# Hash bits for attention masked on TensorE: four 32-column products instead of two full ones, 32-row mask products, and the first weights fetched by SP

## The chip, the cores and the metric

The kernel runs on one core of one Trainium2 chip (trn2). A core has a matrix engine (TensorE, PE in the profile; PEld are its weight loads), a vector engine (VectorE, DVE), an activation engine (ScalarE, ACT), a general engine (GpSimd, POOL) and an engine that mostly issues DMAs (SyncE, SP). Each works through its own queue in order and waits on semaphores for the others. On-chip memory is SBUF (128 partitions); products land in PSUM (128 partitions, in banks).

The metric is device time in microseconds, the median of several runs. The time before the change is 1106.46 us (9 runs, 1104.96 to 1110.92).

## The reference, cut to what matters

Attention with a hash mask, followed by a Fourier mixing block and a two-layer network. Shapes: q, k, v are 4 x 8 x 768 x 64 in float32, `proj` is 64 x 6, the two weights are 512 x 2048 and 2048 x 512 in float64.

```python
q_bits = (np.einsum('bhsd,dk->bhsk', q, proj) > 0)      # 6 bits per query
k_bits = (np.einsum('bhsd,dk->bhsk', k, proj) > 0)      # 6 bits per key
mask = q_bucket[:, :, :, None] == k_bucket[:, :, None, :]  # all six bits equal
scores = np.where(mask, scale * q @ k.T, -1e9)
attn = softmax(scores); x = attn @ v                       # then heads side by side
mixed = np.real(fft(fft(x, axis=1), axis=2))
u = x + mixed
out = u + np.maximum(layernorm(u) @ w_ch1, 0.0) @ w_ch2
```

## The kernel before

**Tiling.** Two heads make a pair, one on partitions 0 to 63 and one on 64 to 127 (a head has 64 dimensions). There are 4 batches of 4 pairs, numbered n = 0 to 15. Queries and keys are 768 long: six tiles of 128 keys (`c`, 0 to 5), and two halves of 384 queries (`g`, `HALF` = 384).

**One key tile.** `weigh(n, c)` makes, for each half g, the scores of both heads in one PSUM tile of two banks (`sc`): products of `kt` and `qt` over 64 partitions for each head (line 869). ACT then takes the exponential into `pk` (line 873). `values` multiplies `pk` of the tile before with v (line 890), and DVE adds up `pk` for the row sums (line 964). At the end of a pair `scale` forms the sums by 32-column products (`sum`, line 908) and divides.

**The mask, in two ways.** Pairs in `LITE` (n = 0 to 4) are masked on TensorE: for each half and head a bf16 product over the hash bits (line 862) is put into the same PSUM tile first, and the scores are added to it. The bits of q are +-0.5 with one more row of -1.5, those of k are +-0.5 with a row of 1, and q's are multiplied by 2^34, so that the sum is 0 where all six bits agree and hugely negative otherwise. Later pairs (n from 5) turn the bits into a bucket number by small products (lines 804, 818, 828), and DVE compares the numbers after the exponential (line 879).

**Bits of a lite pair.** `prepare(n)` runs one pair ahead, a step per key tile. For q and for k, and for each half of the sequence, it multiplies `pjw` (128 x 128, the projection of head h in rows and columns from 64 h) with the transposed input (line 789), and DVE turns the result into bits of both heads, on partitions 0.. and 64.. (line 791; for q also line 796). The tile `qk` holds q's 768 columns and k's 768 columns.

**PSUM buffers.** Products outside the scores and values take a buffer by `pt`. In the first prologue it goes through several pools; afterwards only `ps_1`, with two buffers, serves (line 521). The bits (line 789), the column sums of weights (`ws`, line 656, and `wm`, line 664) and the row sums (line 908) all take turns in these two.

**Weights.** The first weight arrives in float64, as 16 slices of 512 KB. `weights1` converts one slice per key tile in four of five steps: DVE lines 631, 635 and 641, ACT lines 639, 646 and 647. Seven slices are fetched ahead by SP; each further one is fetched into the slot just converted, by POOL (line 701, `Arrival.convert`). Some converted columns are averaged on PE (`ws`, ACT's copy `part` of line 661, `wm`) and centred on DVE (line 670).

**Order of the work.** In batch 0 the order of PE, DVE, ACT and POOL is the order of the program (`manual_schedule`, line 1457). SP's order, and everything later, is set by a scheduler. From batch 1 on, mixing and the network of the batch before (`cs`, `A`, `B`, `un`, `h_p`, `o`) are put between the key tiles. SP also loads q, k and v of the next pair (lines 556, 562, 570), q in eight and k in four transfers of 128-byte pieces.

Of the kernel before, what the change touches and what calls it, by code (L numbers as in the profile page):

```python
# [14 lines left out]
I64 = mybir.dt.int64  # L15
U32 = mybir.dt.uint32
AF = mybir.ActivationFunctionType
ALU = mybir.AluOpType
AX = mybir.AxisListType

P = 128
# [3 lines left out]
DFF = 4 * DM  # L25
# [24 lines left out]
def _consts():  # L50


    s = np.arange(HALF)
    freq = np.concatenate([2 * np.arange(NK), 2 * np.arange(NK) + 1])
    ang = 2.0 * np.pi * (np.outer(s, freq) % S) / S
    seq = np.stack([np.cos(ang), np.sin(ang)])
    seq = seq.reshape(2, NT // 2, P, 2 * NK).transpose(2, 0, 1, 3)


    d = np.arange(DM // 2)  # L60
    ang = 2.0 * np.pi * (np.outer(d, np.arange(DM)) % DM) / DM
    sin = -np.sin(ang)
    sin[0] = 1.0 - 2.0 * (np.arange(DM) % 2)
    chan = np.concatenate([np.cos(ang), sin]).reshape(NDC, P, DM).transpose(1, 0, 2)

    off = np.zeros((P, 2))
    for h in range(2):
        off[h * D : h * D + NBITS] = 0.5  # L70
        off[h * D + NBITS] = (NBITS / 4.0, -1.0)


    pw = np.zeros((P, 2, P))
    for r in range(P):
        h, bit = divmod(r % 32, NBITS)
        if h < 2:
            pw[r, h] = 2.0**bit


    d = np.arange(DM // 2)
    fr = np.concatenate([np.arange(DM // 2 + 1), np.arange(1, DM // 2)])
    ang = 2.0 * np.pi * (np.outer(d, fr) % DM) / DM
    ch = np.where(np.arange(DM) <= DM // 2, np.cos(ang), np.sin(ang))
    ch = ch.reshape(2, P, DM // 2, 2).transpose(1, 0, 3, 2)

    s = np.concatenate([np.arange(2, HALF // 2, 2), np.arange(1, HALF // 2, 2)])  # L90
    rows = np.concatenate([s, [0, HALF // 2], s])
    kind = np.repeat([0, 1, 2, 3], [len(s), 1, 1, len(s)])
    sq = np.zeros((2, 2, P, HALF + 1))
    for par in range(2):
        cols = slice(par * NK, HALF + 1 if par else NK)
        ang = 2.0 * np.pi * (np.outer(rows, freq[: HALF + 1][cols]) % S) / S
        for k in range(2):
            own = kind == (0 if par == k else 3)
            own |= (kind == 1) & (k == 0) | (kind == 2) & (k == par)
            w = np.where(own[:, None], np.sin(ang) if k else np.cos(ang), 0.0)  # L100
            w = w.reshape(NT // 2, P, -1)
            sq[0, k, :, cols] = w[0 if par == k else 2]
            sq[1, k, :, cols] = w[1]
    sq = sq.transpose(2, 0, 1, 3)
    return {
        "pw": np.ascontiguousarray(pw, dtype=np.float32),
        "ch": np.ascontiguousarray(ch, dtype=np.float32),
        "sq": np.ascontiguousarray(sq, dtype=np.float32),
        "seq": np.ascontiguousarray(seq, dtype=np.float32),
        "chan": np.ascontiguousarray(chan, dtype=np.float32),  # L110
        "off": np.ascontiguousarray(off, dtype=np.float32),
    }

# [366 lines left out]
def _main(  # L480
# [27 lines left out]
    def wt(shape, dtype, tag, name, bufs=2):  # L508
        return work.tile(shape, dtype, tag=tag, name=name, bufs=bufs)
# [4 lines left out]
    def pt(shape, name):  # L514

        turn[0] += 1
        if roomy[0] and turn[0] % 2:
            if turn[0] % 4 == 1:
                return ps_o.tile(shape, F32, tag="o", name=name)
            return ps_sc.tile(shape, F32, tag="sc", name=name)  # L520
        return ps_1.tile(shape, F32, tag="ps", name=name)
# [62 lines left out]
    for h in range(2):  # L584
        nc.sync.dma_start(pjw[h * D : (h + 1) * D, h * D : h * D + NBITS], proj)
    off = const.tile([P, 2], F32, tag="off", name="off")
    nc.sync.dma_start(off, cn["off"].ap())
    load(0, "v")
    pj = const.tile([P, 32], F32, tag="pj", name="pj")
    nc.gpsimd.memset(pj, 0.0)  # L590
# [81 lines left out]
    class Arrival:  # L672


        def __init__(self, slices, raws, col):
            self.slices, self.raws, self.col = slices, raws, col
            self.wide = slices[0][1].dtype == I64
            self.depth = len(raws) if self.wide else 4

        def fetch(self, i, queue):  # L680
            if i < len(self.slices):
                dst, src = self.slices[i]
                if self.wide:
                    raw = self.raws[i % self.depth].bitcast(I32)
                    queue.dma_start(raw.bitcast(I64), src)
                else:
                    n = dst.shape[-1]
                    queue.dma_start(
                        dst, src if len(dst.shape) == 2 else src.rearrange("p (s n) -> p s n", n=n)
                    )  # L690

        def convert(self, i, low=None):
            if self.wide:
                dst = self.slices[i][0]
                raw = self.raws[i % self.depth].bitcast(I32)
                if len(dst.shape) == 2:
                    raw = raw.rearrange("p (n w) -> p n w", w=2)
                else:
                    raw = raw.rearrange("p (s n w) -> p s n w", w=2, n=dst.shape[-1])
                narrow(dst, raw, self.col + i, low)  # L700
            self.fetch(i + self.depth, nc.gpsimd)

    def weights1():
        slices = [
            (w1[:, c, f : f + WC], moe_w_ch1[c * P : (c + 1) * P, f : f + WC])
            for f in range(0, DFF, WC)
            for c in range(NDC)
        ]
        zt = wt([P, 3, 2 * WC], F32, "z", "zraw1", 1)
        ft = wt([P, 12, WC], F32, "F", "fraw", 1)  # L710
        raws = [zt[:, i] for i in range(3)] + [
            ft[:, i : i + 2].rearrange("p i w -> p (i w)") for i in range(0, 8, 2)
        ]
        arrival = Arrival(slices, raws, 0)
        for i in range(arrival.depth):
            arrival.fetch(i, nc.sync)
            if i == 1:
                load(1)
        yield
        half = None  # L720
        for i in range(len(slices)):
            arrival.convert(i, ft[:, 8 + i % 4].bitcast(I32))
            yield
            if half:
                centre(half[0], next(half[1]))
                half = None
            if i % NDC == NDC - 1:


                f = i // NDC * WC  # L730
                if f < DFF // 2:
                    half = f, average(f)
                    next(half[1])
# [13 lines left out]
    def prepare(n):  # L747
# [33 lines left out]
        if lite:  # L781


            qk = wt([P, 2, S], BF16, "qb", f"qkb{n}")
            for io, nm in enumerate("qk"):
                for g in range(2):
                    cols = slice(g * HALF, (g + 1) * HALF)
                    ps = pt([P, HALF], f"bits{nm}{n}_{g}")
                    nc.tensor.matmul(ps, pjw, ts[nm][:, cols], start=True, stop=True)
                    bits = qk[:, io, cols]  # L790
                    nc.vector.tensor_scalar(
                        bits, ps, 0.0, off[:, io : io + 1],
                        op0=ALU.is_gt, op1=ALU.subtract,
                    )
                    if io == 0:
                        nc.vector.tensor_scalar(bits, bits, BIG, None, op0=ALU.mult)
                yield
            preps[n] = ts["q"], ts["k"], qk, None
            return
# [50 lines left out]
    def weigh(n, c):  # L850
# [6 lines left out]
        for g in range(2):  # L857
            qs = slice(g * HALF, (g + 1) * HALF)
            ps = ps_sc.tile([P, 2, 512], F32, tag="sc", name=f"sc{n}_{g}_{c}")
            if kb is None:  # L860
                for h, rows in enumerate(heads):
                    nc.tensor.matmul(
                        ps[:, h, 0:HALF], qb[rows, 1, ks], qb[rows, 0, qs],
                        start=True, stop=False,
                    )

            for h, rows in enumerate(heads):
                with behind() if g + h and n >= NPAIR else nullcontext():
                    last[0] = nc.tensor.matmul(  # L869
                        ps[:, h, 0:HALF], kt[rows, ks], qt[rows, qs],  # L870
                        start=kb is not None, stop=True,
                    )
            nc.scalar.activation(  # L873
                pk[:, g, :, 0:HALF], ps[:, :, 0:HALF], AF.Exp, scale=SCALE
            )
# [313 lines left out]
    def weights2():  # L1189

        slices = []
        for half in range(2):
            for r in range(HF // 2):
                for hi, first in ((0, B11), (1, B21)):
# [5 lines left out]
                        (dst[:, first : first + step + 1 : step, r],  # L1200
                         moe_w_ch2[c * P : (c + 1) * P, :])
                    )
        arrival = Arrival(slices, [zt2[:, i] for i in range(2)], NDC * DFF // WC)
        for half in range(2):
            for i in range(arrival.depth) if half == 0 else ():
                arrival.fetch(i, nc.gpsimd)
            for i in range(HF):
                arrival.convert(half * HF + i)
                yield
# [360 lines left out]
```

## Time and profile before

| | |
|---|---|
| median of 9 runs | 1106.46 us |
| the profiled execution | 1105.14 us |
| its span on the core | 1103.4 us |
| mean granted TensorE clock | 0.994 |
| mask products (line 862) | 120, median 323 ns, 11.9 to 155.6 us |
| bits of lite pairs on PE (line 789) | 40 records (two passes a product), median 486 ns |
| evictions of bits on DVE (line 791) | 20, some 0.61 us each |
| scaling of q's bits (line 796) | 10, 0.26 us each |
| weight fetches by POOL (line 685), up to 67.5 us | 9, 0.53 to 0.77 us of POOL each |

A profile is one execution. Its page gives busy time by engine, groups of equal instructions by source line, and the chain of waits that ended last. A timeline row gives the start, the length, the engine, the line, the operation, output and inputs, the shape and the number of merged instructions; brackets give the idle time ahead of the first of them and what ended it. A float32 product appears as two passes. On PE a pass is pipelined: its length includes a tail during which the next one already streams, so what it occupies is read from start to start. "128*32" is the part of the array in use, rows by columns.

### The profile page before, as it was taken

The page shows a single profiled execution, that of the slowest core. Times are in us where ns is not written, and L with a number is a line of the kernel's source. Part 1 is how long each engine was busy: PE and PEld are TensorE (multiplying, and loading weights), DVE is VectorE, ACT ScalarE, POOL GpSimd, SP SyncE. Part 2 cuts the span into 40 slices and gives each one's busy share as a digit, 9 for nine tenths or more (in the row PEclk, how much of TensorE's full clock was granted, in tenths as well). Part 3 has the DMA queues.
Part 4 walks back from the last instruction along what each step waited for, and adds up shares of the span by engine and source line. Part 5 has one row for each costly group of instructions (what it writes and reads, how often), then busy time and mean ns, then how long its engine had stood idle before and what let it go on. Part 6 is the DMA issues. An engine that isn't in the chain of part 4 may idle for free.

```text
span 1103.4 us, 14065 instructions
## 1 busy us (share of the span) xinstructions
PE 1048.8 (95%) x4893; PEld 636.5 (58%) x4893; DVE 790.3 (72%) x1326; ACT 499.6 (45%) x1055; POOL 63.1 (6%) x141
## 2 busy tenths in 40 slices
PE   6989898999989999999999999999999999999996
PEld 3334354445744675545664576645674569768675
DVE  5889968868598977786768785975856785644353
ACT  6978566554267324354426424354315532340420
POOL 1000000002000020010000011001000002100000
PEclk9999999999999999999999999999999999999999
DMA  9845434351055161313144134213032205122401
GB/s 225 210 91 121 81 106 105 119 176 26 20 134 187 66 190 53 63 59 75 26 153 109 49 67 167 44 38 91 20 113 80 66 29 172 53 82 83 127 20 42
DMA packets 175567, 103.13 MB, mean 93 GB/s; under 512 B 129408, under 2 KB 162816, under 8 KB 175488
## 3 DMA queue, kind: packets, MB, share of 16 engines
q1 hardware_dynamic: 168400, 83.93, 28.9%
q0 software_dynamic: 5520, 17.83, 5.3%
q8 instruction: 41, 0.67, 0.3%
q10 hardware_dynamic: 1568, 0.39, 0.2%
q14 instruction: 38, 0.31, 0.1%
HBM read 81.14 MB, written 20.97 MB: 93 GB/s over the span
## 4 chain that ended last, share of the span: by engine, by line
PE 57%; DVE 8%; ACT 3%; issue 1%; DMA 1%; DVEq 0%; ACTq 0%
PE o L1246 20%; PE h_p L1366 19%; PE oo L890 6%; PE sc L869 5%; PE cs L1062 2%; DVE pk L879 2%; PE A L1091 2%; PE B L1091 1%; DVE acc L964 1%; ACT rr L924 1%; DMA zraw<-in_moe_w_ch_dram 1%; PE un L1117 1%; DVE w L1258 1%; PE bits L804 1%; DVE h L1232 1%
## 5 line engine op out<-in xcount | busy, mean ns | idle before, releaser
L1246 PE MATMUL o<-w,h 128*128 128x256 f32 x1152 | 259.4, 382 | 1.1 <-ACT tq L1265 0.7
L1246 PEld LDWEIGHTS o<-w,h 128*128 128x128 f32 x1152 | 216.3, 190 | 43.5 <-issue 4.6
L873 ACT ACTIVATE pk<-sc 128x768 f32<-128x768 f32 x192 | 147.9, 808 | 80.5 <-PE sc L869 62.0
L1366 PE MATMUL h_p<-x,w 128*128 128x384 f32 x448 | 163.5, 495 | 3.9 <-ACT h L1388 2.3
L890 PE MATMUL oo<-pk,vn 128*64 128x385 f32 (+1 forms) x768 | 156.0, 501 | 3.8 <-DVE pk L879 3.3
L869 PE MATMUL sc<-qt,kt 64*128 64x384 f32 x768 | 153.5, 502 | 3.3 <-ACT pk L873 3.0
L879 DVE SCALAR_TENSOR_TENSOR pk<-qb,kb,pk 128x768 f32<-128x768 bf16 x132 | 129.1, 1014 | 29.1 <-ACT pk L873 29.0
L1366 PEld LDWEIGHTS h_p<-x,w 128*128 128x128 f32 x448 | 82.4, 190 | 71.8 <-ACT pk L873 5.4
L964 DVE TENSOR_TENSOR acc<-acc,pk 128x1536 f32<-128x1536 f32 (+1 forms) x72 | 105.9, 1484 | 6.6 <-ACT pk L873 6.1
L1366 PE MATMUL h_p<-w 128*128 128x384 f32 x288 | 105.5, 489 | 2.3 <-ACT w L1403 2.3
L890 PEld LDWEIGHTS oo<-pk,vn 128*64 128x64 f32 x768 | 49.5, 136 | 97.6 <-issue 70.6
L869 PEld LDWEIGHTS sc<-qt,kt 64*128 64x128 f32 x768 | 66.4, 186 | 48.3 <-issue 24.3
L1366 PEld LDWEIGHTS h_p<-w 128*128 128x128 f32 x288 | 53.7, 190 | 41.7 <-ACT w L1403 3.5
L1258 DVE SCALAR_TENSOR_TENSOR w<-o,rs,w 128x256 f32<-128x256 f32 x56 | 26.8, 481 | 41.6 <-PE o L1246 41.6
L1276 ACT COPY tq<-o 128x256 f32<-128x256 f32 x24 | 8.9, 372 | 105.3 <-PE o L1246 105.3
L1246 PE MATMUL o<-w 128*128 128x256 f32 x176 | 42.3, 383 | 1.3 <-DVE w L1258 1.3
L1392 DVE TENSOR_TENSOR h<-h 128x384 f32<-128x384 f32 x32 | 17.8, 556 | 32.7 <-ACT h L1391 32.7
L1265 ACT COPY tq<-o 128x256 f32<-128x256 f32 x24 | 8.9, 371 | 69.3 <-PE o L1246 69.3
L1000 POOL DMA_DIRECT2D out_dram<-w x30 | 16.3, 546 | 388.5 <-issue 293.2
L1246 PEld LDWEIGHTS o<-w 128*128 128x128 f32 x176 | 32.8, 190 | 8.8 <-DVE w L1258 2.9
L1399 DVE TENSOR_TENSOR h<-h 128x384 f32<-128x384 f32 x32 | 17.7, 554 | 26.8 <-ACT h L1398 26.8
L1292 DVE TENSOR_TENSOR tq<-tq,o 128x256 f32<-128x256 f32 x24 | 10.0, 419 | 34.7 <-PE o L1246 34.7
(170 smaller groups left out, 1352.2 us busy)
## 6 DMA issues: line engine op xcount, KB each, us to landing
w<-ad SPq DMA_DIRECT2D x168, 128.0 KB, 2.0
w<-bd SPq DMA_DIRECT2D x42, 512.0 KB, 4.5
zraw<-in_moe_w_ch_dram POOLq DMA_DIRECT2D x21, 512.0 KB, 4.2
bd<-w SPq DMA_DIRECT2D x14, 512.0 KB, 4.0
vn<-in_v_dram SPq DMA_DIRECT2D x32, 192.0 KB, 3.6
qn<-in_q_dram SPq DMA_DIRECT2D x120, 48.0 KB, 2.4
kn<-in_k_dram SPq DMA_DIRECT2D x60, 96.0 KB, 3.5
ad<-tq SPq DMA_DIRECT2D x8, 512.0 KB, 3.0
```

What stands on the lines that cost most here:

```text
L869: last[0] = nc.tensor.matmul(ps[:, h, 0:HALF], kt[rows, ks], qt[rows, qs], start=kb is not None, stop=True,)
L873: nc.scalar.activation(pk[:, g, :, 0:HALF], ps[:, :, 0:HALF], AF.Exp, scale=SCALE)
L879: nc.vector.scalar_tensor_tensor(w, qb[:, h].rearrange("p (g s) -> p g s", g=2), kb[:, h, c : c + 1], w, op0=ALU.is_equal, op1=ALU.mult,)
L890: nc.tensor.matmul(oos[g][h * D : (h + 1) * D, 0:w], nat["v", n][:, (2 * c + h) * D : (2 * c + h + 1) * D], pk[:, g, h, 0:w], start=(c == ...
L964: nc.vector.tensor_tensor(acc[:, g], (first if c == 1 else acc)[:, g], new[:, g], op=ALU.add,)
L1062: nc.tensor.matmul(ps[:, pc + 2 * lo : pc + 2 * hi - 1 : 2], z[:, cp, pc, par, t * P : (t + 1) * P], ch[:, cp, pc, lo:hi], start=(cp == 0) ...
L1091: nc.tensor.matmul(ps[:, cols], F[:, par, k, t, j * P : (j + 1) * P], sq[:, t, k, cols], start=(t == 0), stop=(t == 1),)
L1246: nc.tensor.matmul(ps, a[:, r], right7[i][:, r], start=start and r == 0, stop=r == HF // 2 - 1, skip_group_check=not start,)
L1258: nc.vector.scalar_tensor_tensor(t[:, cols], src, r, t[:, cols], op0=ALU.mult, op1=ALU.add)
L1366: nc.tensor.matmul(ps, left[:, k], right[i][:, k], start=start and k == 0, stop=k == 1, skip_group_check=not start,)
L1392: nc.vector.tensor_tensor(c21, c12, c21, op=ALU.add)
L1399: nc.vector.tensor_tensor(c22, c21, c22, op=ALU.add)
```

## The change

Three things change, for the pairs that are masked on TensorE (n = 0 to 4) and for the first weights:

- The bits of q (and in the same way of k) come from four products of 32 columns, one for each half of the sequence and head, into the four quarters of one PSUM tile of 384 columns, instead of from two products of 128 columns in two PSUM tiles. One eviction on DVE serves all four; the table `off` is laid out for this (`off4`).
- The tile `qk` thus has the first half of the sequence on partitions 0 to 63 and the second on 64 to 127, each head on 32. A query half is multiplied on its own 64 partitions, so the keys' bits are needed on both: two copies on DVE bring each half's key bits to the other half's partitions, in columns 384 to 767. A mask product then runs over 32 rows (before: 64), and for g = 1 the key tiles are found at columns turned by three tiles.
- The fetches of the first weights after the first seven are issued by SP instead of POOL. Those of the second weights stay with POOL.

```diff
@@ _consts
+        "off4": np.ascontiguousarray(np.tile(off[:32], (4, 1)), dtype=np.float32),
@@ _main
-    nc.sync.dma_start(off, cn["off"].ap())
+    nc.sync.dma_start(off, cn["off4"].ap())
@@ class Arrival
-        def __init__(self, slices, raws, col):
-            self.slices, self.raws, self.col = slices, raws, col
+        def __init__(self, slices, raws, col, queue):
+            self.slices, self.raws, self.col, self.queue = slices, raws, col, queue
...
-                    queue.dma_start(raw.bitcast(I64), src)
+                    self.queue.dma_start(raw.bitcast(I64), src)
...
-            self.fetch(i + self.depth, nc.gpsimd)
+            self.fetch(i + self.depth)
@@ weights1
-        arrival = Arrival(slices, raws, 0)
+        arrival = Arrival(slices, raws, 0, nc.sync)
@@ prepare, lite pairs
             qk = wt([P, 2, S], BF16, "qb", f"qkb{n}")
+            bits = {"q": qk[:, 0, 0:HALF], "k": qk[:, 1, 0:HALF]}
             for io, nm in enumerate("qk"):
-                for g in range(2):
-                    cols = slice(g * HALF, (g + 1) * HALF)
-                    ps = pt([P, HALF], f"bits{nm}{n}_{g}")
-                    nc.tensor.matmul(ps, pjw, ts[nm][:, cols], start=True, stop=True)
-                    bits = qk[:, io, cols]
-                    nc.vector.tensor_scalar(
-                        bits, ps, 0.0, off[:, io : io + 1],
-                        op0=ALU.is_gt, op1=ALU.subtract,
-                    )
-                    if io == 0:
-                        nc.vector.tensor_scalar(bits, bits, BIG, None, op0=ALU.mult)
+                ps = pt([P, HALF], f"bits{nm}{n}")
+                for j in range(4):
+                    g, h = divmod(j, 2)
+                    nc.tensor.matmul(
+                        ps[32 * j : 32 * j + 32, :], pjw[:, h * D : h * D + 32],
+                        ts[nm][:, g * HALF : (g + 1) * HALF], start=True, stop=True,
+                    )
+                nc.vector.tensor_scalar(
+                    bits[nm], ps, 0.0, off[:, io : io + 1],
+                    op0=ALU.is_gt, op1=ALU.subtract,
+                )
+                if io == 0:
+                    nc.vector.tensor_scalar(bits[nm], bits[nm], BIG, None, op0=ALU.mult)
+                else:
+                    for g in range(2):
+                        nc.vector.tensor_copy(
+                            qk[g * D : (g + 1) * D, 1, HALF:S],
+                            qk[(1 - g) * D : (2 - g) * D, 1, 0:HALF],
+                        )
                 yield
@@ weigh, lite pairs
-                for h, rows in enumerate(heads):
+                at = (c + (NT // 2 if g else 0)) % NT * P
+                for h in range(2):
+                    rows = slice(g * D + 32 * h, g * D + 32 * h + 32)
                     nc.tensor.matmul(
-                        ps[:, h, 0:HALF], qb[rows, 1, ks], qb[rows, 0, qs],
+                        ps[:, h, 0:HALF], qb[rows, 1, at : at + P], qb[rows, 0, 0:HALF],
                         start=True, stop=False,
                     )
@@ weights2
-        arrival = Arrival(slices, [zt2[:, i] for i in range(2)], NDC * DFF // WC)
+        arrival = Arrival(slices, [zt2[:, i] for i in range(2)], NDC * DFF // WC, nc.gpsimd)
```

In the program, batch 0 keeps its order on PE, DVE, ACT and POOL but for these instructions. On SP the first three further fetches and the fourth go ahead of the loads of q for pair 2, the fifth stands after three of those eight, two more follow the loads of v for pair 2 with a third, and the ninth stands in the middle of q's loads for pair 3.

## The prediction

> **What bounds the kernel now.** I read the page first. TensorE is busy almost everywhere, but the change touches only what runs before about 158 us (the mask products of line 862 begin between 11.9 and 155.6 us), so the rest is needed only to know that a shift there is carried to the end. The busy table of five stretches, then the timelines of PE, DVE and ACT, say what is late in each.
>
> ```profile
> PE 1048.8 (95%) x4893; PEld 636.5 (58%) x4893; DVE 790.3 (72%) x1326; ACT 499.6 (45%) x1055; POOL 63.1 (6%) x141
> ...
> 12.00:41.00 29.00, 26.12 (x164) 11.19 (x164) 20.61 (x32) 23.14 (x41) 2.89 (x5) 1.00 0.96 266
> 41.00:66.00 25.00, 19.96 (x114) 7.96 (x110) 23.13 (x37) 17.73 (x37) 1.58 (x3) 1.00 0.76 144
> 66.00:98.00 32.00, 30.08 (x188) 12.39 (x190) 27.42 (x44) 30.56 (x61) 0.53 (x1) 1.00 0.29 59
> 98.00:122.00 24.00, 22.14 (x140) 8.91 (x136) 22.86 (x41) 15.37 (x32) 0.11 (x1) 1.00 0.57 134
> ```
>
> Columns: stretch, length, busy PE, PEld, DVE, ACT, POOL, clock, DMA share, GB/s. The bound moves: ACT and DMA in pair 0, DVE in pair 1 (23.1 of 25), ACT in pair 2 (30.6 of 32), DVE and PE together in pair 3. Nowhere is one engine alone the limit, so a saving counts only where its engine is late. The sharpest place is the end of pair 1:
>
> ```profile
> 56.59 1.51 PE L890 MATMUL oo<-pk,vn 128*64 128x385 f32 x8
> 59.95 1.74 PE L789 MATMUL bitsk<-kt,pjw 128*128 128x384 f32 x4 [1.84 <-DVE qkb L791]
> 63.33 1.06 PE L656 MATMUL ws<-w,ones 128*32 128x512 f32 x8 [1.65 <-DVE qkb L791]
> ...
> 59.28 0.61 DVE L791 TENSOR_SCALAR qkb<-bitsq,off 128x384 bf16<-128x384 f32 x1
> 59.93 0.26 DVE L796 TENSOR_SCALAR qkb<-qkb 128x384 bf16<-128x384 bf16 x1
> ...
> 64.46 0.58 ACT L661 COPY part<-ws 128x512 f32<-128x512 f32 x1 [6.94 <-PE ws L656]
> ```
>
> PE holds two PSUM buffers for these products. The two halves of q's bits fill both, so k's bits wait for DVE, the column sums (`ws`) wait again, and ACT stands idle for 6.94 us behind them. The same wait at k's bits comes back at 114.21 (1.48 us).
>
> **Part 1, bits in four column products.** Before, one of q or k takes two full products: from 53.38 to the next work at 54.87, 1.49 us. Four 32-column products side by side are in the trace for the later pairs:
>
> ```profile
> 141.67 0.52 PE L804 MATMUL bits<-qt,pj 128*32 128x384 f32 x2
> 141.69 0.52 PE L804 MATMUL bits<-kt,pj 128*32 128x384 f32 x2
> 142.02 0.49 PE L804 MATMUL bits<-qt,pj 128*32 128x384 f32 x2
> 142.03 0.49 PE L804 MATMUL bits<-kt,pj 128*32 128x384 f32 x2
> 142.45 1.99 PE L1062 MATMUL cs<-ch,z 128*128 128x256 f32 x8
> ```
>
> All four end in 142.45 - 141.67 = 0.78 us. PE saves 0.71 us for each of q and k, ten times: 7.1 us. DVE: q goes from 1.65 us (59.28 to 60.93: two evictions, two scalings) to half, saving 0.82 per pair. k goes from two evictions (62.66 to 63.71, 1.05) to one eviction (about 0.6) and two half-partition bf16 copies. No such copy is in the trace; nearest is line 796 (bf16 in SBUF, same length), which takes 0.18 from start to start. Bounds: 0.1 (a copy does less than a scaling) and 0.6 (the price of an eviction). I take 0.18, being the same length and type: k saves about 0.1, at worst it loses 0.8. Each of q and k holds one PSUM buffer instead of two.
>
> **Part 2, mask products on 32 rows.** Per key tile and query half there are still two bf16 products of 384 columns, side by side as before (the hash products of line 818 show that 32-row ones run in pairs too: four in 0.43 us). Duration of one does not change. What changes is the shape of the array between neighbours. Now mask and score products both use 64 rows; afterwards 32, then 64. The timeline prices a change of shape:
>
> ```profile
> 73.96 0.33 PE L862 MATMUL sc<-qkb 64*128 64x384 bf16 x2
> 74.12 0.81 PE L869 MATMUL sc<-qt,kt 64*128 64x384 f32 x4
> 74.86 1.51 PE L890 MATMUL oo<-pk,vn 128*64 128x385 f32 x8
> ```
>
> Four score passes followed by the value products (128*64) take 74.86 - 74.12 = 0.74 us; followed by a mask product of their own shape (73.31 to 73.96) they take 0.65. So 0.09 us per change of shape. The Trainium skill, TensorEngine Tiling (Array Packing), section Tiling Modes, says that a change of tiling mode, and not of the tile alone, drains TensorE; it gives no figure, and counted by tiles alone (still two at once) the part would cost 0. By the row each key tile has three more changes (mask to score twice, score to mask once): 0.27 us, over 5 pairs x 6 tiles 8.1 us of PE. No 32-to-64 change is in the trace. Bounds: 0 (the array need not drain) and 0.35 (the tail of a score pass, 0.16, since the four passes' 0.81 is one start distance of 0.32 and a last pass of 0.49; plus an open weight load, 0.19 in the group rows). I take 0.09, since it is also what 32 to 128 rows costs at line 818 (0.25 from the start of a product that streams 0.16). On PE alone parts 1 and 2 thus cancel (-7.1, +8.1); the gain must come from waits.
>
> **Part 3, fetches on SP.** Nine weight fetches leave POOL (0.53 us each, POOL 6% busy: worth nothing) and join SP, each waiting for the conversion that frees its slot. The page Trainium Kernel Development and Optimization, Key Constraints, says that queues of all engines share the same DMA engines and a second issuer saves only sequencer time; here the rule speaks against the move, as what queues behind on SP matters. In the order of the changed program three loads of q for pair 2 stand behind the fetch that waits for conversion 3, and five more, with four of k and two of v, behind conversion 4 (ended near 39.4). They are needed at 50.30 (q) and 54.79 (k). At the light price (eight issues in 3.92 us at 51.71) the five q loads are issued by 42 and land (2.6 us) before 46: hidden. At the loaded price (15.06 us for eight at 23.09) q lands near 52, about 2 us late. The weights are fetched some 20 us before their conversion (fetched 52.85, used 88.66), so nothing waits for those. One gain: POOL's fetch at 17.13 no longer shares the DMA with the one that ACT awaits at 24.80 (2.18 us idle).
>
> **The sum** (minus is gain), along what is late:
> - Start to 27.8: four bits side by side and fewer evictions put the first mask about 0.8 us earlier; ACT leads and at 24.80 waits for DMA, so this needs that fetch earlier too. 0 to -2.5, taken -1.0.
> - 27.8 to 41, PE without gaps: three key tiles +0.8, one set of bits -0.7: +0.1.
> - 58 to 69: bits of k run at 58.0, `ws` starts when q's single eviction ends (59.95), tile 5 about 61, value products to 64.4, `wm` at 64.4 instead of 67.49: -3.1. DVE keeps up (its line 670 waits for `wm`). What is late next is ACT's chain, which starts with `ws`.
> - 69 to 81, ACT-bound: the extra PE time fits in PE's 1.92 us gap at 81.46: 0.
> - 81 to 98, PE-bound: five tiles +1.4, two bits -1.4: 0.
> - 98 to 122, DVE-bound: q's bits -0.8, k's -0.1: -0.9.
> - 122 to 158, pair 4: DVE first, then PE from 146 with two tiles: +0.6.
>
> Total -4.3 us. Afterwards the order of work is nearly the same and the chain of waits runs on PE, so it carries. The profiled execution took 1105.14 us (span 1103.4), becoming 1100.8; it lay 1.3 below the median, from which 1106.46 - 4.3 = **1102.2 us**.
>
> **Rivals.**
> - No drain between 32 and 64 rows: 10 PE-bound tiles at 0.27 are given back, -2.8 more: 1099.4. For it: both are row tilings. Against: every change of shape in the trace pays. 12%.
> - The waits at 59.95 and 63.33 go, but DVE (no idle time from 41.4 to 66.3) or late q loads take their place; only a third of that gain remains: about 1105. 21%.
> - Slower: the 32-to-64 change costs a whole emptying of the array and an open weight load. With some 14 tiles on the path, 14 x 3 x (s - 0.09) eats 4.3 us from s = 0.19 on. At s = 0.30, +4.5: 1111. 9%. For it: it happens 90 times and is untested. Against: the 0.09 does not grow with the load's size.
> - Forecast and its neighbourhood, 1100 to 1104: 58%.
>
> A difference under 0.2% (2.2 us) can't be told from none. Faster: the first rival, most of the forecast, a little of the second: 0.68. Same: 0.19. Slower: 0.13, including SP's delay at the loaded price with a bad drain. Range 1098.8 to 1107.5: down to the first rival, up to the second's worst.
>
> **What would show it.** In the changed profile: the bits' group at 0.78 us per four; no PE wait on the eviction of q's bits; ACT's 6.94 us idle gone to about 3.5; mask to score starts 0.25 apart instead of 0.17; `wm` near 63.5. Wrong would be: starts over 0.35 apart, DVE waiting for q or k of pair 2, or copies over 0.4 us.

## The result, and the profile after

The changed kernel takes 1103.24 us (median of 10 runs, 1100.53 to 1104.05). Against runs of the kernel before taken on the same chip the ratio is 0.9965, 95% interval 0.9954 to 0.9976: faster by 2.7 to 5.1 us, where 4.3 had been forecast. A second set of 11 runs (e8 below) gives 0.9975 [0.9958, 0.9991]. The profiled execution took 1103.1 us, its span 1101.3 us; the span before was 1103.4 us.

Line numbers have moved: the bits are now line 794 (789 before) and their eviction 798 (791), mask products 878 (862), scores 885 (869), values 906 (890), `ws` 658 (656), `wm` 666 (664).

The busy row of the changed kernel's page:

```profile
PE 1057.9 (96%) x4933; PEld 630.0 (57%) x4933; DVE 786.5 (71%) x1321; ACT 500.2 (45%) x1055; POOL 58.4 (5%) x132
```

And its table by stretch, for the same four stretches and with the same columns as in the prediction:

```profile
12.00:41.00 29.00, 28.70 (x172) 9.43 (x170) 20.07 (x32) 24.75 (x43) 0.00 (x0) 1.00 0.85 266
41.00:66.00 25.00, 23.68 (x137) 7.74 (x136) 23.38 (x38) 20.71 (x42) 0.00 (x0) 1.00 0.59 132
66.00:98.00 32.00, 31.66 (x198) 10.79 (x198) 27.48 (x46) 30.26 (x60) 0.00 (x0) 1.00 0.47 84
98.00:122.00 24.00, 23.09 (x149) 7.56 (x146) 21.88 (x40) 14.74 (x37) 0.11 (x1) 1.00 0.63 135
```

PE's busy time has risen in every stretch, from 26.1, 20.0, 30.1 and 22.1 us to 28.7, 23.7, 31.7 and 23.1. Over the whole page it rises by 9.1 us (from 1048.8) while the span falls by 2.1: PE work was added, and waits went. The waits of PE between 12 and 135 us (what waited, for whom; total, times, longest) say which ones. Before (the four longest):

```profile
PE sc L862 <- ACT pk L873: 6.3, 5, 1.9
PE bitsk L789 <- DVE qkb L791: 3.3, 2, 1.8
PE ws L656 <- DVE qkb L791: 1.6, 1, 1.6
PE wm L664 <- ACT part L661: 1.1, 1, 1.1
```

After:

```profile
PE ws L658 <- DVE qkb L798: 0.9, 1, 0.9
PE wm L666 <- ACT part L663: 0.9, 1, 0.9
PE sc L878 <- ACT pk L889: 0.7, 2, 0.4
```

The wait of k's bits for a PSUM buffer is gone, and most of PE's waiting for ACT is gone too (e1 below shows that longer key tiles alone bring that from 6.3 to 1.5 us). The end of pair 1 in the timelines of PE, DVE and ACT (start, length):

```profile
57.09 0.85 PE L794 MATMUL bitsk<-kt,pjw 128*32 128x384 f32 x8
58.88 1.06 PE L658 MATMUL ws<-w,ones 128*32 128x512 f32 x8 [0.94 <-DVE qkb L798]
63.55 1.12 PE L666 MATMUL wm<-part,mean 128*128 128x512 f32 x2
...
58.22 0.61 DVE L798 TENSOR_SCALAR qkb<-bitsq,off 128x384 bf16<-128x384 f32 x1
61.42 0.52 DVE L806 COPY qkb<-qkb 64x384 bf16<-64x384 bf16 x2
61.98 0.43 DVE L633 TENSOR_SCALAR w<-zraw 128x512 int32<-128x512 int32 x1
...
60.02 0.58 ACT L663 COPY part<-ws 128x512 f32<-128x512 f32 x1 [3.44 <-PE ws L658]
```

`bitsk` starts without brackets, so nothing holds it up; `ws` starts at 58.88 instead of 63.33 and still waits 0.94 us for the one eviction of q's bits, which ends at 58.83. ACT's idle time is 3.44 instead of 6.94 us. The two copies of k's bits take 0.56 us from start to start (61.42 to 61.98), 0.28 each.

Now a key tile that follows another without a gap, in PE's timeline of the changed kernel:

```profile
69.70 0.33 PE L878 MATMUL sc<-qkb 32*128 32x384 bf16 x2
69.97 0.92 PE L885 MATMUL sc<-qt,kt 64*128 64x384 f32 x4
70.82 0.33 PE L878 MATMUL sc<-qkb 32*128 32x384 bf16 x2
71.08 0.92 PE L885 MATMUL sc<-qt,kt 64*128 64x384 f32 x4
71.93 1.51 PE L906 MATMUL oo<-pk,vn 128*64 128x385 f32 x8
73.37 0.34 PE L878 MATMUL sc<-qkb 32*128 32x384 bf16 x2
```

From mask to mask with both halves and the values: 73.37 - 69.70 = 3.67 us. The same pieces took 3.17 us before (73.14 to 76.31). So a tile costs 0.50 us more, not 0.27. The starts of PE and of its weight loads (PEld) show why. Before:

```profile
73.14 0.34 PE L862 MATMUL sc<-qkb 64*128 64x384 bf16 x2
76.31 0.34 PE L862 MATMUL sc<-qkb 64*128 64x384 bf16 x2
...
73.14 0.36 PEld L869 LDWEIGHTS sc<-qt,kt 64*128 64x128 f32 x4
```

After:

```profile
69.97 0.30 PEld L885 LDWEIGHTS sc<-qt,kt 64*128 64x128 f32 x4 [0.17 <-issue]
```

Mask to score is 0.27 (before 0.16 to 0.17), the expected drain of 0.1. But four score passes now span 0.92 and not 0.81, because the first pass is 0.11 longer. It is the pass behind the change of shape. Before, the load of its float32 weights started with the mask product (73.14), 0.17 us ahead of the pass; now it starts with the pass itself (69.97), so nothing hides it. Two changes to 64 rows cost 0.10 + 0.11 each, the one back to 32 costs 0.09: 0.51 in sum. The kernel before already held this price, in a place that the prediction did not read (PE's timeline, a score product behind one of 128 rows):

```profile
172.60 0.81 PE L1091 MATMUL B<-sq,F 128*128 128x192 f32 x4
173.35 0.92 PE L869 MATMUL sc<-qt,kt 64*128 64x384 f32 x4
```

### The profile page after: what moved, and what is told of

It is laid out like the page before. It is cut to its first block, busy times and chain, and to the rows that moved or that the text cites. A ratio compares the mean times of both kernels' runs of the same rounds, so it can differ in the third digit from the quotient of the medians.

```text
span 1101.3 us, 14127 instructions
## 1 busy us (share of the span) xinstructions
PE 1057.9 (96%) x4933; PEld 630.0 (57%) x4933; DVE 786.5 (71%) x1321; ACT 500.2 (45%) x1055; POOL 58.4 (5%) x132
## 4 chain that ended last, share of the span: by engine, by line
PE 61%; DVE 11%; ACT 4%; issue 2%; DMA 2%; DVEq 0%; SPq 0%; ACTq 0%
PE o L1262 22%; PE h_p L1382 19%; PE oo L906 6%; PE sc L885 6%; DVE pk L895 3%; PE cs L1078 2%; PE A L1107 2%; DMA zraw<-in_moe_w_ch_dram 2%; PE B L1107 1%; DVE acc L980 1%; ACT rr L940 1%; DVE w L1274 1%; DVE h L1248 1%; PE bits L817 1%; PE un L1133 1%
## 5 line engine op out<-in xcount | busy, mean ns | idle before, releaser
L885 PE MATMUL sc<-qt,kt 64*128 64x384 f32 x768 | 159.8, 519 | 3.9 <-ACT pk L889 3.6
L885 PEld LDWEIGHTS sc<-qt,kt 64*128 64x128 f32 x768 | 62.9, 185 | 54.6 <-issue 29.7
```

The source lines that it names most:

```text
L885: last[0] = nc.tensor.matmul(ps[:, h, 0:HALF], kt[rows, ks], qt[rows, qs], start=kb is not None, stop=True,)
```

## The experiments

Each kernel was timed beside the kernel before; "before" in the expectations is that kernel, "shift" is how much later (minus: earlier) the same PE instruction starts than in the profile of before.

**e1: mask products on 32 rows alone.** The kernel before; only the rows of the mask products that carry bits are used, everything else stays.

```diff
-                for h, rows in enumerate(heads):
+                for h in range(2):
+                    rows = slice(h * D, h * D + 32)
```

> The kernel before, with one edit: a mask product takes 32 rows (0 to 31 or 64 to 95) instead of 64; bits, copies and fetches stay as before. If the changes of shape cost what the trace after the change shows, about 0.5 us for a key tile (three drains of 0.09, and 0.11 twice for a first float32 weight load that nothing hides), some 10 to 13 tiles on the path make it 5 to 6.5 us slower: 1111 to 1113. If only the drains count, as predicted (0.27 a tile): about 3 us slower, 1109 to 1110. If 32 and 64 rows need no drain: 0.

Measured: 1107.7 us against 1105.55, ratio 1.002 [1.001, 1.0031], or 1.1 to 3.4 us slower. By the time alone the smaller price (about 3 us) is nearer. In its profile each tile back to back adds 0.5 us (the shift is +2.5, +3.0 and +3.5 at 70, 75 and 78 us); it reaches +5.7 at 110 and +4.9 us at 155 us, where the last mask products run. 30 tiles at 0.5 are 15 us of PE; the rest fills waits (PE waits 1.5 us for ACT instead of 6.3, and 1.0 for q's bits instead of 3.3). Later the shift falls to +4.0 at 180 us and to +1.8 at 250; the second step comes where the profile of before has its second interval at half clock (from 231 us) and this one has none. So the 5 to 6.5 us were there in this profile where the change acts, and the forecast was too high for the end.

**e2: fetches on SP alone.** The kernel before with the first weights' later fetches issued by SP.

```diff
-            self.fetch(i + self.depth, nc.gpsimd)
+            self.fetch(i + self.depth, nc.sync if self.col == 0 else nc.gpsimd)
```

> The kernel before, with one edit: the first weights' later fetches are issued by SP. If the earlier landing of the third slice carries part of the gain: ACT's 2.18 us wait near 24.8 nearly gone, key tile 4 of pair 0 some 1.9 us earlier, time 1 to 2 us lower (1104.5 to 1105.5). Rival, the move is hidden (weights are fetched some 20 us ahead): no change. Rival, the move carries the whole gain: about 1103.

Measured: 1105.08 us, ratio 0.9993 [0.998, 1.0006], no difference that can be told. The timeline of ACT shows what the part does, the slice awaited in pair 0:

```profile
22.62 0.69 ACT L639 ACTIVATE fraw<-zraw 128x512 int32<-128x512 uint32 x1 [0.33 <-DMA zraw<-in_moe_w_ch_dram]
```

ACT stood idle for 0.33 us here, before for 2.18 (at 24.80). The shift is -2.1 at 28 us and -1.7 from 37 to 80, then 0.0 behind an interval at half clock at 80 us, and -2.2 at 250, behind the second such interval of the profile of before. The early gain is in this profile, but the medians do not show it, and e8 below leaves open how much of it is due to SP.

**e3: the changed kernel with these fetches back on POOL** (bits and mask products alone).

```diff
-            self.fetch(i + self.depth)
+            self.fetch(i + self.depth, nc.gpsimd)
```

> The changed kernel with the later fetches of the first weights back on POOL. If bits and masks carry most of the gain: 1104.5 to 1105, with ACT waiting about 2 us for the third slice again and the waits on q's eviction still gone. If SP carries all: 1106 or more. If SP carries nothing: 1103.2.

Measured: 1104.31 us, ratio 0.9986 [0.9976, 0.9995]. Shift -3.3 at 63 and at 146 us: the gain at the end of pair 1 is here without SP. ACT waits 0.92 us for its third slice, not the 2 expected. That profile (span 1106.9) then holds 17 us at half clock, so its end says nothing. Multiplied with e2's ratio it gives 0.998, which lies in the interval of e8 and just above that of the first result; the parts add up as far as can be told.

**e4: two PSUM buffers again.** The changed kernel, with the same four 32-column products for q (and k), but each sequence half in its own buffer with its own eviction.

```diff
-                ps = pt([P, HALF], f"bits{nm}{n}")
+                pss = [pt([P, HALF], f"bits{nm}{n}_{g}") for g in range(2)]
...
+                for g in range(2):
+                    part = slice(g * D, (g + 1) * D)
                     nc.vector.tensor_scalar(
-                        bits[nm], ps, 0.0, off[:, io : io + 1],
+                        bits[nm][part], pss[g][part], 0.0, off[part, io : io + 1],
```

> The changed kernel, but the four bit products of q (and of k) go into two PSUM tiles, two products each, evicted one after the other, as many evictions as before. PE's time for bits stays at the new level. If the freed PSUM buffer is what gains: k's bits and the column sums wait again near 58 to 64 and some 3 us are lost, 1106 to 1107. If the shorter products are what gains: 1103 to 1104.

Measured: 1110.96 us, ratio 1.0046 [1.0029, 1.0064], slower than the kernel before and some 8 to 9 us slower than the changed one by their ratios, more than expected. The timelines of PE and DVE:

```profile
60.14 1.50 PE L794 MATMUL bitsk<-kt,pjw 128*32 128x384 f32 x8 [1.71 <-DVE qkb L800]
63.47 1.07 PE L658 MATMUL ws<-w,ones 128*32 128x512 f32 x8 [1.83 <-DVE qkb L800]
64.46 0.44 PE L880 MATMUL sc<-qkb 32*128 32x384 bf16 x2
64.83 1.65 PE L887 MATMUL sc<-qt,kt 64*128 64x384 f32 x4
...
59.48 1.26 DVE L800 TENSOR_SCALAR qkb<-bitsq,off 64x384 bf16<-64x384 f32 x2
62.80 1.27 DVE L800 TENSOR_SCALAR qkb<-bitsk,off 64x384 bf16<-64x384 f32 x2
```

Both waits are back at about their old length (1.84 and 1.65 before), although the products are those of the changed kernel. Each wait ends with the first of two evictions (at 60.08 for q, 63.41 for k), not with the second: PE waits for a free buffer, not for both evictions to be done. So the gain at the end of pair 1 comes from the buffer that q no longer holds, not from the shorter products. By 63 us the shift is +0.1, where the changed kernel has -3.4 and -4.5 in its two profiles. The last line of PE shows the rest: four score passes take 1.65 us instead of 0.92, since PE runs at half clock for 6.8 us right behind these waits; at 69 us the shift is +4.0.

**e5, e6, e7: no change of shape.** The changed kernel with its bits in the order head, half, so that a head's 64 partitions hold both halves. Mask products use 64 rows again; q's bits are scaled into two copies, each with the other half's 32 rows at zero, and k's bits are copied in four pieces of 32 partitions, by POOL (e5), DVE (e6) or ACT (e7).

```diff
-                    g, h = divmod(j, 2)
+                    h, g = divmod(j, 2)
...
-                    nc.vector.tensor_scalar(bits[nm], bits[nm], BIG, None, op0=ALU.mult)
+                    for g in range(2):
+                        nc.vector.tensor_scalar(
+                            qk[:, 0, g * HALF : (g + 1) * HALF], raw, sel[:, g : g + 1],
+                            None, op0=ALU.mult)
...
+                    for j in range(4):
+                        nc.gpsimd.tensor_copy(
+                            qk[32 * j : 32 * j + 32, 1, HALF:S],
+                            qk[32 * (j ^ 1) : 32 * (j ^ 1) + 32, 1, 0:HALF])
...
-                    rows = slice(g * D + 32 * h, g * D + 32 * h + 32)
+                    rows = heads[h]
```

> The changed kernel, but the mask products keep 64 rows: bits of one head and both halves lie on partitions 64h+32g, the query half that a product is not for has its other 32 rows zeroed by a per-partition factor, and GpSimd makes the four copies of k's bits. So no change of shape between mask and score products. If the 0.50 us per key tile that the changed kernel pays (3.67 instead of 3.17 us back to back) is the cause of the missing gain, ten key tiles on the path (three of pair 0, five of pair 2, two of pair 4) are given back: about 5 us faster than the changed kernel, 1098 to 1099, mask to score start 0.165 us, a key tile 3.17 us. By the 0.27 us of the prediction: 2.7 faster, about 1100.5. If the tiles are hidden beside other engines, or GpSimd's copies come late: 1103 or more, with a PE wait on GpSimd at the first mask of a pair.

> As e5, but VectorE makes the four copies of k's bits. Per pair VectorE has two scalings of q (0.2 more) and four copies of 0.28 instead of two (0.56 more). In pairs 1 and 3, where VectorE is late, 0.8 each: about 1.5 us slower than e5, 1100 if e5 is at 1098.5. If the copies are hidden there: same as e5 within 0.5 us. If a 32-partition copy costs less than the 0.28 us of a 64-partition one, below that.

> As e5, but ScalarE makes the four copies of k's bits. ScalarE is late in pair 2 (30.6 of 32 us busy) and in pair 0: four copies at 0.3 us add 1.2 us there each: 1 to 2.5 us slower than e5. If ScalarE's idle time in front of the value products covers them: same as e5.

> The changed kernel once more, beside e5 to e7 on the same chip: 1103.2 us, ratio to the kernel before 0.9965. Its own key tiles take 3.67 us again. If intervals of half clock vary from one execution to the next, their number and places differ from the first profile of this kernel, and the profiled span moves by 1.7 us for each 3.4 us of them.

Measured, on one chip (before 1106.27 us):

| | median us | ratio to before |
|---|---|---|
| e5, copies by POOL | 1106.98 | 1.001 [1.0, 1.0021] |
| e6, copies by DVE | 1101.41 | 0.9952 [0.9936, 0.9969] |
| e7, copies by ACT | 1122.2 | 1.0144 [1.0122, 1.0166] |
| e8, the changed kernel | 1102.79 | 0.9975 [0.9958, 0.9991] |

The key tile falls as expected, here in PE's timeline of e6's kernel in a second profile (e10):

```profile
68.32 0.34 PE L887 MATMUL sc<-qkb 64*128 64x384 bf16 x2
68.49 0.81 PE L894 MATMUL sc<-qt,kt 64*128 64x384 f32 x4
69.14 0.33 PE L887 MATMUL sc<-qkb 64*128 64x384 bf16 x2
69.30 0.81 PE L894 MATMUL sc<-qt,kt 64*128 64x384 f32 x4
70.04 1.51 PE L915 MATMUL oo<-pk,vn 128*64 128x385 f32 x8
71.48 0.34 PE L887 MATMUL sc<-qkb 64*128 64x384 bf16 x2
```

3.16 us, and four score passes are 0.81 again. But where the copies go decides the result. e6, expected behind e5, came first, and even it is only 1.4 us below e8, where about 3.5 was expected: PE waits 5.6 us for ACT's exponentials ahead of masks up to 165 us, in e8 1.7. PE's waits in e5 (what waited, for whom; total, times, longest):

```profile
PE sc L887 <- POOL qkb L815: 4.5, 6, 1.2
PE ws L662 <- DVE qraw L803: 1.9, 1, 1.9
```

ACT's timeline in e7:

```profile
90.04 1.49 ACT L898 ACTIVATE pk<-sc 128x768 f32<-128x768 f32 x2
95.64 2.07 ACT L815 COPY qkb<-qkb 32x384 bf16<-32x384 bf16 x4 [4.11 <-DVE qkb L803]
97.73 0.66 ACT L645 ACTIVATE fraw<-fraw 128x512 int32<-128x512 uint32 x1
```

POOL needs 0.49 to 0.87 us a copy (2.64 us for four at 12.04), and PE waits for it; that profile has five intervals at half clock, those of the changed kernel two and one. On ACT the four copies cost 2.07 us, but the wait ahead of them costs more: ACT works in order, and behind the copy that waits 4.11 us for DVE stand the conversions and exponentials. The wait sums to 18.6 us over five pairs. The expectation had priced only the copies' own length. On DVE nothing has to wait for another engine's result, and a 32-partition copy takes 0.25 us, the same as one of 64.

**e9: masks of both halves first.** The changed kernel, its 32-row mask products kept, but the two halves' products one behind the other, then both halves' scores; e10 is e6 once more.

```diff
+        def mask(g):
+            ps = pss[g] = ps_sc.tile([P, 2, 512], F32, tag="sc", name=f"sc{n}_{g}_{c}")
+            if kb is None:
...
+        if kb is None:
+            mask(0)
+            mask(1)
         for g in range(2):
...
...
-            if kb is None:
-                at = (c + (NT // 2 if g else 0)) % NT * P
...
```

> The changed kernel, but the mask products of both query halves of a key tile are issued before its score products, so that a tile has one change from 32 to 64 rows instead of two and none back. If the price is 0.093 us per change and 0.107 for the first float32 weight load after it, a tile back to back falls from 3.67 us by 0.29 to 3.38, and ten tiles on the path give 2.9 us: about 1100. Rival: the second mask product needs the second PSUM buffer before the first scores run, so TensorE waits for ScalarE's exponentials where two tiles follow one another: waits on ScalarE of several us, and no gain, 1103 or more.

> The kernel of e6 once more, beside e9 on the same chip: 1101.4 us, ratio to the kernel before 0.995; a key tile 3.17 us. If the two half-clock intervals near 113 and 140 us took back 3.4 us in the first profile, a profile without them shows a shift of 6 to 7 us at 158 us instead of 4.3; if the gain of the key tiles was lost to waits on VectorE and ScalarE in pair 4, the shift at 158 us is 4.3 again, whatever the clock.

Measured, against 1106.58 us: e9 1101.99 us, ratio 0.9948 [0.9929, 0.9967]; e10 1101.91 us, ratio 0.9949 [0.9932, 0.9966]. PE's timeline of e9:

```profile
85.84 0.34 PE L878 MATMUL sc<-qkb 32*128 32x384 bf16 x4
86.11 1.56 PE L893 MATMUL sc<-qt,kt 64*128 64x384 f32 x8
87.60 1.51 PE L914 MATMUL oo<-pk,vn 128*64 128x385 f32 x8
89.05 0.34 PE L878 MATMUL sc<-qkb 32*128 32x384 bf16 x4
```

A tile takes 3.21 us, less than the 3.38 expected. Two changes of shape and one open weight load are gone (0.29), and there is a gain that the expectation missed: the four 32-row products lie on different rows and all four run within 0.34 us, as two did before (0.17 more). The rival is there in part, 5.8 us of PE waits for ACT's exponentials in ten places (0.7 and 1.7 in the two profiles of the changed kernel), and does not eat the gain.

The changed kernel's own second profile (e8) has the key tile at 3.67 us again and, before its last 10 us, a single interval at half clock of 3.4 us, where the first had 10.2 us. Its span is 1099.9 us, 1.4 shorter. At half speed, so 1.7 us for each 3.4, it should have been up to 3.4 shorter. The start took back 1.1 of this: at 29.5 us the shift is -0.3, in the first profile -1.4, and at 158 us -2.4 against -3.5. From there to the end e8 does better by 2.5 us, with 6.8 us less at half clock.

That start bears on the move to SP. ACT's wait for its third slice in e8 (fetches by SP) and in e3 (by POOL):

```profile
23.91 0.69 ACT L641 ACTIVATE fraw<-zraw 128x512 int32<-128x512 uint32 x1 [0.85 <-DMA zraw<-in_moe_w_ch_dram]
23.99 0.69 ACT L641 ACTIVATE fraw<-zraw 128x512 int32<-128x512 uint32 x1 [0.92 <-DMA zraw<-in_moe_w_ch_dram]
```

The two are alike, and their shifts agree within 0.1 us from 20 to 146 us. In the nine profiles with SP this wait ends at 22.6 to 23.9 us or there is none; in the three with POOL (before, e1, e3) it ends at 24.0 to 24.8. That the slice lands earlier with SP is likely; a gain in time from it is not shown.

e6, e9 and e10 have lower medians than the changed kernel (1101.4 to 1102.0 against 1102.8 and 1103.2) and are the best seen here; their intervals overlap with its own, so that they beat the kernel before is shown, and that they beat the changed one is likely.

e10 also settles what was lost in e6 behind 118 us. Its shift at 158 us is -5.8, e6's -4.3. The row of the table by stretch for 118 to 158 us, of e6:

```profile
118.00:158.00 40.00, 35.99 (x212) 19.84 (x210) 27.03 (x43) 22.13 (x46) 1.32 (x2) 0.96 0.39 93
```

The same row of e10:

```profile
118.00:158.00 40.00, 35.82 (x219) 19.25 (x216) 29.21 (x48) 23.86 (x51) 1.32 (x2) 1.00 0.41 97
```

The program is the same, and so is the wait in question (PE waits 1.9 us for DVE's `bt` in both profiles); the clock, 0.96 against 1.00, is not. Both shifts are -5.9 at 135 us, so of e6's two intervals, at 113 and 141 us, only the second counts: from 135 to 158 us e6 loses 1.6 us, e10 0.1. The expectation for a profile without half clock was 6 to 7.

## Why the prediction was right, step by step

How the shift of PE's instructions develops in the two profiles of the changed kernel, beside the terms of the sum:

| stretch, us | predicted | measured | again (e8) |
|---|---|---|---|
| start to 27.8 | -1.0 | -1.9 | -0.8 |
| 27.8 to 41 | +0.1 | +0.8 | +0.8 |
| 41 to 53 | not in the sum | +0.4 | +0.3 |
| 53 to 69 | -3.1 | -3.2 | -3.2 |
| 69 to 81 | 0 | -0.1 | -0.1 |
| 81 to 98 | 0 | +0.6 | +0.6 |
| 98 to 122 | -0.9 | -1.1 | -1.1 |
| 122 to 158 | +0.6 | +1.0 | +1.0 |
| to 158 | -4.3 | -3.5 | -2.4 |
| 158 to the end | 0 | +1.4 | -1.1 |

- **The mechanism held.** Four products of bits take 0.78 us (52.64 to 53.42), as read from the later pairs. The gain is the PSUM buffer at the end of pair 1, at the place and of the size named; `wm` starts at 63.55 where "near 63.5" was forecast. e4 shows that it is the buffer. Of the signs named, ACT's idle time (3.44 us) and the start of mask to score (0.27) came as forecast; PE's wait on the eviction of q's bits did not go, but fell to 0.94 us at `ws`, as the sum itself had it.
- **The term that was mis-sized** is the 0.09 us taken for a change of shape, 0.27 per tile. It measured 0.50, because two of the three changes also leave a float32 weight load open (0.11 each). It is the cause of the plus in 27.8 to 41 (three tiles at 0.5 less one set of bits at 0.7 give just the +0.8), of the +0.6 in 81 to 98 (four tiles at 0.5 less two sets of bits), and of 122 to 158 (two tiles, +1.0). In 41 to 53 three tiles add 1.5, of which PE's waits for ACT take up the most; the sum had left this stretch out. The upper bound of 0.35 for a change had an open weight load in it; the value was chosen from a row in which bf16 or value products follow, and the row at 173.35 that has a float32 score pass behind another shape was not looked up. The rule of the Trainium skill that a change of tiling mode drains TensorE (TensorEngine Tiling (Array Packing), Tiling Modes) agrees with the trace (some 0.1 us at each change): counted by tiles alone the tile would have stayed at 3.17 us. The rival without a drain is out.
- **The near hit is in part luck.** With 0.50 for a tile and four tiles in 81 to 98 the same sum gives -2.6 instead of -4.3. The first profile makes up 0.9 of this at the start; e8's does not, and stands at -2.4 at 158 us.
- **The start** gave 0.9 more than taken in the first profile and 0.2 less in e8's. ACT's wait for its third slice shrank from 2.18 to 0.24 us, in e8 to 0.85; with 0.92 in e3, by POOL, how much of this is due to SP stays open. The first mask itself came 0.5 and 0.05 us earlier, not 0.8; PE waits there for k's eviction. The range of 0 to -2.5 for this term held both.
- **Readings that were off.** The stretch 81 to 98 holds four key tiles (at 81.46, 86.12, 90.77 and 93.93), not five. DVE is not without idle time from 41.4 to 66.3: it waits 0.80 us for ACT ahead of 65.66. In the pair quoted for the weights (52.85 and 88.66) the lead is 36 us, not 20; that nothing waits for them holds all the more.
- **SP's queue** did no harm: the five loads of q behind conversion 4 take 2.49 us from 38.37, 0.5 each, the light price, and neither PE nor DVE waits for any of them.
- **The copies** cost 0.28 us, not 0.18; what it costs at the end was not measured by itself.
- **Carried to the end** was the weakest claim. From 158 us on, the order of the work is the same, but the intervals at half clock are not: 6.8 and 3.4 us in the changed kernel's first profile, 3.4 in its second, twice 3.4 in that of before. By 200 us the first had lost 1.2 us. The forecast is a median of runs over which these intervals vary, so the profiled pair alone could not have confirmed it.

## What to carry to other kernels

Count the PSUM buffers that a step holds before its instructions: a packed product that needs one buffer instead of two removed the waits, and with the old number of buffers (e4) the same packed products and masks were slower than the kernel before. Price a change of array shape with the first weight load behind it, and put products of equal shape side by side; on different rows they even overlap. When work is moved to an engine with spare time, count what stands behind its wait in that engine's order, not its own length.

## What the runs showed of the hardware

Before a kernel's last 10 us, the profile's clock rows go to half for 3.41 us or twice that at a time, in a kernel whose PE is 96% busy. Such intervals begin on a grid: in the profile of before 51.2 us apart, in that of after 54.6, whole multiples (15 and 16) of 3.413 us. I laid this grid over twelve profiles, from 20 us behind the first product to 300 us, and took PE's busy share in the interval ahead of each:

| busy share of the interval ahead | intervals | of these at half clock |
|---|---|---|
| under 0.42 | 11 | 11 |
| 0.42 to 0.50 | 23 | 16 |
| 0.50 to 0.60 | 32 | 3 |
| over 0.60 | 887 | 7, each the second of a double |

So over 2 us without products within one interval were followed by half clock every time, 1.7 to 2 us in 16 of 23 cases, and where the grid lies differs from execution to execution: the same wait is followed by half clock in e6 and not in e10, 1.5 us apart at 158 us. The spread of the kernel before, 1101.4 to 1111.7 us beside e5 to e8, fits this. The Trainium skill (TensorE: Matmul & The Clock Gate, Part 1: The HAM clock gate) describes this window of 3413 ns, free-running, with full clock lost after an idle window; the length and the free phase agree, but here windows that were 0.42 to 0.50 busy were mostly enough. The link of low activity and half clock is a regularity of these profiles; no run here filled a wait with idle products to force it.
